# Spacing the feed-forward weight chunks and word buffers 32 bytes further apart

## The chip, the cores and the metric

The kernel runs on one core of a Trainium2 chip. The metric is device time in microseconds (us), as the median of timed runs of the whole program. A core has a matrix engine (PE, with its weight loads shown apart as PEld), a vector engine (DVE), a scalar engine (ACT), a general engine (POOL) and a queue engine that issues DMAs (SP).

## The reference

The program computes a long convolution (as a product of Fourier transforms), gates it with its input, and sends every token through a feed-forward network with squared ReLU:

```python
h_filt = (np.maximum(pos_emb @ w1, 0.0) @ w2) * window      # filter, 12480 x 128
u = x * v                                                   # 4 batches, 12480 x 128
y = irfft(rfft(u, 2 * S) * rfft(h_filt, 2 * S), 2 * S)[:S]
t = (x * y).reshape(49920, 128)
h = np.maximum(t @ w_in, 0.0)                               # 128 x 2048
out = h * h @ w_out                                         # 2048 x 128
```

## The kernel before

The convolution of each of the four batches is done in four stages of small fp32 matrix products (`s1` to `s4`, two-dimensional transforms over a 112 x 112 grid in the buffer `W`). The feed-forward network runs over 98 groups of up to 512 tokens; each group takes eight steps `f`. After the first batch, the transform stages of the next batch are woven between the feed-forward steps: a step issues its products, and in between it advances the generator of the stages by one. Once all batches are transformed, the last stretch (here "the tail", from about 2620 us on) holds feed-forward steps alone.

To keep fp32 accuracy at the speed of the short format, every operand of the feed-forward network is split into a high and a low word (fp32r tiles), and each product is three: high by high, low by high, high by low. That is the helper `mm3`, lines 95, 96 and 97. Its first argument is the stationary operand (loaded into PE by a weight load ahead of the product), its second the moving one:

```python
nc.tensor.matmul(o, lh, rh, start=first, stop=False)   # line 95
nc.tensor.matmul(o, ll, rh, start=False, stop=False)   # line 96
nc.tensor.matmul(o, lh, rl, start=False, stop=last)    # line 97
```

The stationary operands are the feed-forward weights. They lie in 16 chunks `wt[0]` to `wt[15]` of 2048 bytes for each partition, eight of `w_in` and eight of `w_out`; a chunk holds 1024 bytes of high words and 1024 of low words, and `wi(k, h, f)` picks 128 columns of one. A chunk first holds the raw 64-bit weights (tile `raw`, loaded by `load_weights`) and is then overwritten by its converted words (tile `wt`, made by `convert_weights` from temporaries `cv`).

The moving operands are words of tokens, `zh` and `zl` (two buffers each, made by `zsplit`), against `w_in` into PSUM tile `A` (`m_h`), and words of squared activations, `gh` and `gl` (two buffers each, made by `m_g` and `m_l`, 4096 bytes for two sub-tiles), against `w_out` into PSUM tile `O` or, in the tail, `F` (`m_o`). In the tail every odd step takes its `r`, `gh` and `gl` from a second pool `tp` that lies elsewhere, on the left side of memory. One step is twelve products: six `A<-zh/zl` and six `O<-gh/gl`. ACT makes the ReLU and the squares, DVE the low words (line 818), and both run behind PE.

Products of one engine run in the order of the code. While one product streams its moving operand out of SBUF, the load of the next product's weights is running. Two reads of SBUF are therefore always going on at the same time: the moving words of this product and the weights of the next. Below, the *offset* of a product is the SBUF byte address of the weights that are loaded under it minus that of its own moving words, modulo 256.

Of the kernel before, what the change touches and what calls it, by code (L numbers as in the profile page):

```python
# [8 lines left out]
F32R = mybir.dt.float32r  # L9
F16 = mybir.dt.float16  # L10
I32 = mybir.dt.int32
# [5 lines left out]
D = 128  # L17
# [9 lines left out]
GT = NT // NG  # L27
NS = NF // 2
GM = 512
# [9 lines left out]
TH = 4  # L39
CW = 256  # L40
NCW = DFF // CW


@with_exitstack
def hyena_moe_kernel(
# [34 lines left out]
    def pool(name, side="left", **kw):  # L80
        return tc.tile_pool(name=name, bufs=kw.pop("bufs", 2), side=side, reuse_waits="tile", **kw)
# [17 lines left out]
    def load_weights(wp):  # L99
        raws = []  # L100
        for c in range(2 * NCW):
            raw = wp.tile([128, CW, 2], I32, tag="w", name="raw", bufs=2 * NCW)
            src = (w_in if c < NCW else w_out).bitcast(I32)[:, c % NCW * 2 * CW : (c % NCW + 1) * 2 * CW]
            nc.sync.dma_start(out=raw.rearrange("p a b -> p (a b)"), in_=src)
            raws.append(raw)
        return raws

    def convert_weights(p, wp, raws, wt, chunks):
        V = nc.vector
        for c in chunks:  # L110
            low, high = raws[c][:, :, 0], raws[c][:, :, 1]
            mag, top, sgn = (p.tile([128, CW], I32, tag=k, name="cv") for k in ("cm", "ct", "cs"))
            mf = mag.bitcast(F32)
            tf = top.bitcast(F32)
            V.tensor_scalar(out=top, in0=high, scalar1=0x7FFFFFFF, scalar2=None, op0=ALU.bitwise_and)
            yield
            V.tensor_scalar(out=mf, in0=tf, scalar1=2.0**-15, scalar2=122880.0, op0=ALU.max, op1=ALU.min)
            yield
            V.tensor_scalar(out=top, in0=mag, scalar1=3, scalar2=0x7FFFFFFF, op0=ALU.logical_shift_left, op1=ALU.bitwise_and)
            yield  # L120
            V.tensor_scalar(out=mag, in0=low, scalar1=1, scalar2=None, op0=ALU.logical_shift_right)
            nc.gpsimd.tensor_copy(mf, mag)
            yield
            V.tensor_scalar(out=sgn, in0=high, scalar1=-0x80000000, scalar2=0x40000000, op0=ALU.bitwise_and, op1=ALU.bitwise_xor)
            yield
            V.tensor_tensor(out=top, in0=top, in1=sgn, op=ALU.bitwise_xor)
            wt[c] = wp.tile([128, 2, CW], F32R, tag="w", name="wt", bufs=2 * NCW)
            hi12, lo12 = wt[c][:, 0, :], wt[c][:, 1, :]
            nc.gpsimd.tensor_copy(hi12, tf)
            yield  # L130
            V.tensor_scalar(out=sgn, in0=top, scalar1=-0x800000, scalar2=None, op0=ALU.bitwise_and)
            yield
            V.scalar_tensor_tensor(out=mf, in0=mf, scalar=2.0**-51, in1=sgn.bitcast(F32), op0=ALU.mult, op1=ALU.mult)
            yield
            V.tensor_sub(out=tf, in0=tf, in1=hi12.bitcast(F32))
            yield
            V.tensor_add(out=lo12, in0=tf, in1=mf)
            yield
# [546 lines left out]
    def run(gen):  # L685
        for _ in gen:
            pass
# [6 lines left out]
    def take(name, *args, **kw):  # L694
        held[name] = ExitStack()
        return held[name].enter_context(pool(name, *args, **kw))
# [39 lines left out]
    wp = ctx.enter_context(pool("wp", "right"))  # L736
    wt = {}
    tabs = [take(k, "right").tile([128, TH * TC, 2, I], F32, name=k, bufs=1) for k in ("tbb", "tba")]
    for k in range(2 * TH):
        table(t2h, k, tabs[k < TH])  # L740
    raws = load_weights(wp)
    run(s1f)
    s1 = stage1(0, True, "right", during_s1)
    cvp = take("cvp")
    conv = [convert_weights(cvp, wp, raws, wt, range(k, 2 * NCW, 2)) for k in range(2)]
    run(stage2(True, True, "left", during_s2f))
    ft = []
# [4 lines left out]
    held["tbb"].close()  # L752

    mp = ctx.enter_context(pool("mp", "right"))
    head = [mp.tile([D, GM], F32R, tag=k, name=k)[:, :GT] for k in ("zh", "zl")]
    s4 = stage4(0, done, take("t1p"))
    run(stage3(True, ft[0], lambda t: t == -12 and step(s4)))
    idle(12)
# [1 line left out]
    def wi(k, h, f):  # L760
        return wt[k * NCW + f // 2][:, h, f % 2 * 128 : (f % 2 + 1) * 128]

# [13 lines left out]

    def zsplit(zi):
        n = zi.shape[1]
        hi = mp.tile([D, GM], F32R, tag="zh", name="zh")[:, :n]
        lo = mp.tile([D, GM], F32R, tag="zl", name="zl")[:, :n]  # L780
        nc.scalar.copy(hi, zi)  # L781
        nc.gpsimd.tensor_sub(out=lo, in0=zi, in1=hi.bitcast(F32))  # L782
        return hi, lo
# [7 lines left out]
    def m_g(A, p, n, between, way):  # L791

        r = p.tile([128, 2, GM], F32, tag="r", name="r")[:, :, :n]
        hi = p.tile([128, 2, GM], F32R, tag="gh", name="gh")[:, :, :n]
        h = A[:, :, :n]
        nc.scalar.activation(r, h, AF.Relu)  # L799
        between()  # L800
        if way != "b":
            nc.scalar.activation(hi, r, AF.Square)  # L802
        if way == "p":
            nc.vector.scalar_tensor_tensor(out=h, in0=h, scalar=0.0, in1=r, op0=ALU.max, op1=ALU.mult)  # L804
            return p, h, hi, way
        nc.scalar.activation(r, r, AF.Square)  # L806
        return p, r, hi, way

    def m_l(st, share):
        p, g, hi, way = st  # L810
        lo = p.tile([128, 2, GM], F32R, tag="gl", name="gl")[:, :, : g.shape[2]]
        if way == "b":
            nc.vector.tensor_copy(hi, g)  # L813
        if share:
            nc.gpsimd.tensor_sub(out=lo[:, 1, :], in0=g[:, 1, :], in1=hi[:, 1, :].bitcast(F32))
            nc.vector.tensor_sub(out=lo[:, 0, :], in0=g[:, 0, :], in1=hi[:, 0, :].bitcast(F32))
        else:
            nc.vector.tensor_sub(out=lo, in0=g, in1=hi.bitcast(F32))  # L818
        return hi, lo
# [51 lines left out]
    for i in range(NM):  # L871
        for f in range(NS):
            adv(1)
            A = m_h(zT, f)
            last = m_o(*pend.pop(0)) if len(pend) > 1 else None
            adv(2)
            if not nxt[0] and not tail:
                tail.append(ctx.enter_context(pool("tp")))
            late.append((i, f, m_g(A, tail[0] if tail and f % 2 else mp, GN[i], lambda: m_out(last), way(i * NS + f))))
            while len(late) > len(tail):  # L880
                x, y, st = late.pop(0)
                pend.append((x, y, m_l(st, False)))
            if i + 1 < NM:
                if f == (1 if i else 3):
                    ready(i + 1)
                    zi = zload(i + 1)
                if f == (4 if i else 6):
                    nzT = zsplit(zi)
            adv(3)
            n = i * NS + f  # L890
            if stage[0] != since[0]:
                since = stage[0], n + 4
            owed += EXTRA[done[1] > 0]
            if owed >= 1 and stage[0] in (("s3", "s4") if done[1] else ("s2", "s3", "s4")) and nxt[0] == 1 and n >= since[1]:
                owed -= 1
                since = stage[0], n + 3
                for k in range(1, 4):
                    adv(k)
        if i + 1 < NM:
            zT = nzT  # L900
    for x, y, st in late:
        pend.append((x, y, m_l(st, True)))
# [114 lines left out]
```

## Time and profile before

| | |
|---|---|
| timed runs | 3122.88, 3111.55, 3119.26 us; median 3119.26 us |
| profiled execution, first to last instruction | 3112.0 us (the only time that the profile gives for it) |
| PE busy | 3072.7 us, 99% of the span |
| PEld, DVE, ACT, POOL busy | 83%, 82%, 78%, 48% |
| chain that ended last | PE 92% |
| granted TensorE clock | 0.999 of full speed over the span |

The timed runs are 11 us apart, 0.4% of the time. The busy share of PE counts overlapping products once, so the spacing of the products, not their durations, has to be read to see how fast PE goes. A product's duration runs from its start to the end of its results and is longer than the spacing to the next start (389 against 227 ns in a stretch shown below); a difference of durations between two products of the same shape is a difference of spacing.

### The profile page before, as it was taken

How to read it: one execution, taken by the hardware profiler on the slowest of the kernel's cores; microseconds unless marked ns; L12 is line 12 of the kernel's file. 1: busy time of each engine (PE TensorE's matmuls, PEld its weight loads, DVE VectorE, ACT ScalarE, POOL GpSimd, SP SyncE). 2: the span in 40 equal slices, each digit the busy share in tenths (PEclk: the TensorE clock that was granted, in tenths of full speed). 3: DMA queues.
4: the chain of work that ended last, by engine and by line, in shares of the span. 5: the costliest groups of instructions: out<-in, count | busy, mean ns of one | idle time of the engine just before them, and what ended most of it. 6: DMA issues, size and time to landing. Idle time of an engine off the chain costs nothing.

```text
span 3112.0 us, 49107 instructions
## 1 busy us (share of the span) xinstructions
PE 3072.7 (99%) x16086; PEld 2579.8 (83%) x16086; DVE 2538.0 (82%) x3080; ACT 2419.1 (78%) x3130; POOL 1501.6 (48%) x1631
## 2 busy tenths in 40 slices
PE   9989999999999999999999999999999999999999
PEld 7767888888888888888888888888888888888887
DVE  7888898878877988878877898878877799777776
ACT  5556777777788777788888877787788887878787
POOL 1249765556544565546644575646644466000000
PEclk9999999999999999999999999999999999999999
DMA  5783574434200664434300375434410176100000
GB/s 184 263 294 99 137 166 137 124 111 145 67 21 15 151 161 132 130 91 127 115 15 21 80 176 144 133 92 121 124 51 14 36 168 156 33 24 24 24 26 20
DMA packets 342623, 323.11 MB, mean 104 GB/s; under 512 B 161968, under 2 KB 288800, under 8 KB 342368
## 3 DMA queue, kind: packets, MB, share of 16 engines
q1 hardware_dynamic: 313216, 272.25, 30.2%
q0 software_dynamic: 29152, 47.72, 6.4%
q8 instruction: 128, 2.10, 0.3%
q14 instruction: 127, 1.04, 0.1%
HBM read 231.78 MB, written 65.60 MB: 96 GB/s over the span
## 4 chain that ended last, share of the span: by engine, by line
PE 92%; POOL 2%; DMA 2%; DVE 2%; issue 1%; ACT 1%; SPq 0%; DVEq 0%; ACTq 0%; POOLq 0%
PE A L95 11%; PE A L97 11%; PE A L96 11%; PE O L97 9%; PE O L96 9%; PE O L95 9%; PE F L380 6%; PE F L492 6%; PE F L293 5%; PE F L97 4%; PE F L95 4%; PE F L96 4%; PE A L290 2%; PE A L291 1%; POOL W L405 1%
## 5 line engine op out<-in xcount | busy, mean ns | idle before, releaser
L799 ACT ACTIVATE r<-A 128x1024 f32<-128x1024 f32 (+2 forms) x784 | 803.8, 1025 | 420.8 <-PE A L97 407.0
L818 DVE TENSOR_TENSOR gl<-r,gh 128x1020 fp32r<-128x1020 f32 (+1 forms) x433 | 642.5, 1484 | 113.9 <-ACT r L806 80.0
L95 PE MATMUL A<-zh,wt 128*128 128x512 f32 (+2 forms) x1568 | 671.4, 428 | 0.9 <-DVE gl L818 0.9
L97 PE MATMUL A<-zl,wt 128*128 128x512 f32 (+2 forms) x1568 | 613.8, 391 | 0.0
L96 PE MATMUL A<-zh,wt 128*128 128x512 f32 (+2 forms) x1568 | 612.9, 391 | 0.0
L802 ACT ACTIVATE gh<-r 128x1024 fp32r<-128x1024 f32 (+2 forms) x461 | 486.9, 1056 | 62.8 <-PE O L96 57.2
L97 PE MATMUL O<-gl,wt 128*128 128x512 f32 (+2 forms) x1248 | 487.4, 391 | 4.2 <-DVE gl L818 4.2
L96 PE MATMUL O<-gh,wt 128*128 128x512 f32 (+2 forms) x1248 | 485.0, 389 | 0.0
L95 PE MATMUL O<-gh,wt 128*128 128x512 f32 (+2 forms) x1248 | 484.9, 389 | 0.0
L804 DVE SCALAR_TENSOR_TENSOR A<-A,r 128x1024 f32<-128x1024 f32 (+2 forms) x350 | 425.4, 1215 | 68.1 <-ACT r L799 66.5
L818 DVE TENSOR_TENSOR gl<-A,gh 128x1024 fp32r<-128x1024 f32 (+2 forms) x350 | 426.1, 1218 | 63.1 <-ACT gh L802 20.4
L806 ACT ACTIVATE r<-r 128x1020 f32<-128x1020 f32 (+1 forms) x434 | 460.3, 1061 | 12.5
L813 DVE CAST gh<-r 128x1020 fp32r<-128x1020 f32 (+1 forms) x323 | 225.6, 698 | 221.2 <-ACT r L806 152.7
L782 POOL TENSOR_TENSOR zl<-zi,zh 128x512 fp32r<-128x512 f32 (+2 forms) x97 | 126.4, 1303 | 522.4 <-ACT zh L781 506.1
L567 POOL TENSOR_TENSOR al<-W,ah 112x512 fp32r<-112x512 f32 x214 | 281.9, 1318 | 189.2 <-ACT ah L561 185.0
L501 POOL TENSOR_TENSOR W<-c 112x224 f32<-112x224 f32 x256 | 217.6, 861 | 285.7 <-ACT c L499 275.0
L97 PEld LDWEIGHTS A<-zl,wt 128*128 128x128 f32 x1568 | 294.6, 188 | 64.7
L95 PEld LDWEIGHTS A<-zh,wt 128*128 128x128 f32 x1568 | 295.5, 188 | 51.4 <-DVE gl L818 3.1
L96 PEld LDWEIGHTS A<-zh,wt 128*128 128x128 f32 x1568 | 296.2, 189 | 45.1
L417 POOL TENSOR_TENSOR W<-W,m 112x256 f32<-112x256 f32 x168 | 177.8, 1058 | 247.3 <-DVE m L415 233.1
L97 PEld LDWEIGHTS O<-gl,wt 128*128 128x128 f32 x1248 | 234.2, 188 | 54.5 <-DVE gl L818 5.9
L96 PEld LDWEIGHTS O<-gh,wt 128*128 128x128 f32 x1248 | 234.2, 188 | 50.6
(127 smaller groups left out, 5495.3 us busy)
## 6 DMA issues: line engine op xcount, KB each, us to landing
ht<-Hd SPq DMA_DIRECT2D x224, 256.0 KB
tb<-t POOLq DMA_DIRECT2D x224, 196.0 KB, 3.1
xt<-x SPq DMA_DIRECT2D x224, 112.0 KB
xt<-xs SPq DMA_DIRECT2D x96, 224.0 KB
vt<-vs SPq DMA_DIRECT2D x96, 224.0 KB
tb<-t2s SPq DMA_DIRECT2D x168, 112.0 KB
Hd<-he SPq DMA_DIRECT2D x28, 512.0 KB
zd<-zs SPq DMA_DIRECT2D x222, 64.0 KB
```

Of the source, the lines that this page charges most:

```text
L95: nc.tensor.matmul(o, lh, rh, start=first, stop=False)
L96: nc.tensor.matmul(o, ll, rh, start=False, stop=False)
L97: nc.tensor.matmul(o, lh, rl, start=False, stop=last)
L380: nc.tensor.matmul(U[:I, k * 256 : (k + 1) * 256], tb[:KP, k, :], a[:, k], start=True, stop=True)
L501: nc.gpsimd.tensor_sub(out=dst[:, 1], in0=c[:, :, 0:3:2], in1=c[:, :, 3:0:-2])
L567: eng.tensor_sub(out=lo, in0=w, in1=hi.bitcast(F32))
L799: nc.scalar.activation(r, h, AF.Relu)
L802: nc.scalar.activation(hi, r, AF.Square)
L804: nc.vector.scalar_tensor_tensor(out=h, in0=h, scalar=0.0, in1=r, op0=ALU.max, op1=ALU.mult)
L806: nc.scalar.activation(r, r, AF.Square)
L813: nc.vector.tensor_copy(hi, g)
L818: nc.vector.tensor_sub(out=lo, in0=g, in1=hi.bitcast(F32))
```

## The change

`WP = 8` words (32 bytes) are added behind each of the first 15 weight chunks, behind each `zh` and `zl` buffer and behind each `gh` and `gl` buffer. So that a chunk keeps its place, the 16 buffers of one ring become 16 rings of one buffer each. The views into the tiles are those of before, so every instruction reads and writes the same shapes.

```diff
+WP = 8
 ...
-            raw = wp.tile([128, CW, 2], I32, tag="w", name="raw", bufs=2 * NCW)
+            raw = wp.tile([128, 2 * CW + WP * (c < 2 * NCW - 1)], I32, tag=f"w{c}", name="raw", bufs=1)[:, : 2 * CW].rearrange("p (a b) -> p a b", b=2)
 ...
-            wt[c] = wp.tile([128, 2, CW], F32R, tag="w", name="wt", bufs=2 * NCW)
+            wt[c] = wp.tile([128, 2 * CW + WP * (c < 2 * NCW - 1)], F32R, tag=f"w{c}", name="wt", bufs=1)[:, : 2 * CW].rearrange("p (a b) -> p a b", a=2)
 ...
-    head = [mp.tile([D, GM], F32R, tag=k, name=k)[:, :GT] for k in ("zh", "zl")]
+    head = [mp.tile([D, GM + WP], F32R, tag=k, name=k)[:, :GT] for k in ("zh", "zl")]
 ...
-        hi = mp.tile([D, GM], F32R, tag="zh", name="zh")[:, :n]
-        lo = mp.tile([D, GM], F32R, tag="zl", name="zl")[:, :n]
+        hi = mp.tile([D, GM + WP], F32R, tag="zh", name="zh")[:, :n]
+        lo = mp.tile([D, GM + WP], F32R, tag="zl", name="zl")[:, :n]
 ...
-        hi = p.tile([128, 2, GM], F32R, tag="gh", name="gh")[:, :, :n]
+        hi = p.tile([128, 2 * GM + WP], F32R, tag="gh", name="gh")[:, : 2 * GM].rearrange("p (t n) -> p t n", t=2)[:, :, :n]
 ...
-        lo = p.tile([128, 2, GM], F32R, tag="gl", name="gl")[:, :, : g.shape[2]]
+        lo = p.tile([128, 2 * GM + WP], F32R, tag="gl", name="gl")[:, : 2 * GM].rearrange("p (t n) -> p t n", t=2)[:, :, : g.shape[2]]
```

In the built programs the addresses, modulo 256, come out so:

| buffers | before | after |
|---|---|---|
| weight chunks 0 to 7 (`w_in`) and 8 to 15 (`w_out`) | all 224 | 0, 32, 64, ... 224 for each eight |
| `zh`, `zl` (two buffers each) | all 224 | 0 and 32, 64 and 96 |
| `gh`, `gl` (two buffers each) | all 224 | 128 and 160, 192 and 224 |
| `gh`, `gl` of the tail's second pool | all 128 | 128 and 160, 192 and 224 |
| everything else on the right side (tables and buffers of the first stages, `r`, `zi`, `ot`) | | moved by 32 modulo 256 as a whole |

There are 8861 feed-forward products that are followed by another feed-forward product. Counted in the built program, their offsets are:

| offset | 0 | 32 | 64 | 96 | 128 | 160 | 192 | 224 |
|---|---|---|---|---|---|---|---|---|
| before | 8364 | 0 | 0 | 497 | 0 | 0 | 0 | 0 |
| after | 1514 | 683 | 1483 | 763 | 1486 | 679 | 1485 | 768 |

No instruction moves on any engine. On PE, at one of the places where a step's products against `w_out` (`gh`, `gl`) are followed by a product of stage 4 (`ah`, `tb`), before:

```order
L95 MATMUL O<-gh,wt 128x510
L96 MATMUL O<-gh,wt 128x510
L97 MATMUL O<-gl,wt 128x510
L95 MATMUL O<-gh,wt 128x510
L96 MATMUL O<-gh,wt 128x510
L97 MATMUL O<-gl,wt 128x510
L95 MATMUL F<-ah,tb 112x256
```

The changed program has the same rows in the same places, each with a line number that is one higher; the other engines agree in the same way. What differs is which engines a few instructions wait for, since chunks now lie in other places over memory that the filter's first stage has left. On SP, the loads of the raw chunks before:

```order
L104 DMA raw<-w_in 128x512 [waits DMAHW4_49]
L104 DMA raw<-w_in 128x512 [waits DMAHW5_49,PE_49,Activation_49]
L104 DMA raw<-w_in 128x512 [waits DMAHW6_49]
L104 DMA raw<-w_in 128x512 [waits DMAHW7_49,Pool_49]
L104 DMA raw<-w_in 128x512 [waits DMAHW0_49]
L104 DMA raw<-w_in 128x512 [waits DMAHW1_49]
```

The same six loads after the change:

```order
L105 DMA raw<-w_in 128x512 [waits DMAHW4_49]
L105 DMA raw<-w_in 128x512 [waits DMAHW5_49]
L105 DMA raw<-w_in 128x512 [waits DMAHW6_49]
L105 DMA raw<-w_in 128x512 [waits DMAHW7_49]
L105 DMA raw<-w_in 128x512 [waits DMAHW0_49,DVE_49,PE_49]
L105 DMA raw<-w_in 128x512 [waits DMAHW1_49,Pool_49]
```

The waits for PE, ACT and POOL have moved from the second and fourth load to the fifth and sixth; the queue's order is that of before.

## Rows read from the trace of the kernel before

**Rows 1.** The page: span, busy engines, granted clock, chain by engine.

```profile
span 3112.0 us, 49107 instructions
...
PE 3072.7 (99%) x16086; PEld 2579.8 (83%) x16086; DVE 2538.0 (82%) x3080; ACT 2419.1 (78%) x3130; POOL 1501.6 (48%) x1631
...
PEclk9999999999999999999999999999999999999999
...
PE 92%; POOL 2%; DMA 2%; DVE 2%; issue 1%; ACT 1%; SPq 0%; DVEq 0%; ACTq 0%; POOLq 0%
```

**Rows 2.** Groups of PE by line: busy us, mean ns of one, idle before.

```profile
L95 PE MATMUL A<-zh,wt 128*128 128x512 f32 (+2 forms) x1568 | 671.4, 428 | 0.9 <-DVE gl L818 0.9
L97 PE MATMUL A<-zl,wt 128*128 128x512 f32 (+2 forms) x1568 | 613.8, 391 | 0.0
...
L97 PE MATMUL O<-gl,wt 128*128 128x512 f32 (+2 forms) x1248 | 487.4, 391 | 4.2 <-DVE gl L818 4.2
L96 PE MATMUL O<-gh,wt 128*128 128x512 f32 (+2 forms) x1248 | 485.0, 389 | 0.0
L95 PE MATMUL O<-gh,wt 128*128 128x512 f32 (+2 forms) x1248 | 484.9, 389 | 0.0
...
L96 PE MATMUL F<-gh,wt 128*128 128x510 f32 x320 | 125.5, 392 | 0.0
```

**Rows 3.** Who PE waited for: us in total, times, longest.

```profile
PE F L380 <- DVE W L387: 7.9, 23, 2.2
```

**Rows 4.** PE in order of time: start, duration; six 512-column products at offset 0.

```profile
1004.61 0.39 PE L95 MATMUL O<-gh,wt 128*128 128x512 f32 x1
...
1005.98 0.26 PE L492 MATMUL F<-ft,v 112*112 112x112 f32 x1
```

**Rows 5.** PE in order of time, tail: six products at offset 96, then six at 0.

```profile
2900.59 0.40 PE L95 MATMUL F<-gh,wt 128*128 128x510 f32 x1
...
2901.99 0.39 PE L95 MATMUL A<-zh,wt 128*128 128x510 f32 x1
...
2903.36 0.39 PE L95 MATMUL F<-gh,wt 128*128 128x510 f32 x1
...
2904.72 0.39 PE L95 MATMUL A<-zh,wt 128*128 128x510 f32 x1
```

**Rows 6.** Groups of PE at 397.1, 909.8, 499.25, 1022.3 us: one product each.

```profile
L97 PE MATMUL O<-gl,wt 128*128 128x512 f32 x1 | 0.4, 396 | 0.0
...
L97 PE MATMUL O<-gl,wt 128*128 128x512 f32 x1 | 0.4, 391 | 0.0
...
L97 PE MATMUL O<-gl,wt 128*128 128x512 f32 x1 | 0.4, 397 | 0.0
...
L97 PE MATMUL O<-gl,wt 128*128 128x512 f32 x1 | 0.4, 389 | 0.0
```

**Rows 7.** In order of time at 503.33 us: a last product, the load beneath.

```profile
503.33 0.40 PE L97 MATMUL O<-gl,wt 128*128 128x512 f32 x1
503.33 0.61 PEld L293 LDWEIGHTS F<-ef,ut 112*120 112x120 f32 x3
```

**Rows 8.** Groups of PE at 1936.3, 2025.7, 1978.9, 1907.8, 2080.7 us: one product each.

```profile
L97 PE MATMUL O<-gl,wt 128*128 128x510 f32 x1 | 0.4, 389 | 0.0
...
L97 PE MATMUL O<-gl,wt 128*128 128x510 f32 x1 | 0.4, 395 | 0.0
...
L97 PE MATMUL O<-gl,wt 128*128 128x510 f32 x1 | 0.4, 388 | 0.0
...
L97 PE MATMUL O<-gl,wt 128*128 128x510 f32 x1 | 0.4, 387 | 0.0
...
L97 PE MATMUL O<-gl,wt 128*128 128x510 f32 x1 | 0.4, 397 | 0.0
```

**Rows 9.** Tile raw, by operation: duration min/median/max, first and last start.

```profile
L115 DVE TENSOR_SCALAR cv<-raw x16: 285/286/290, 85.5 to 137.4; 128x256 int32<-128x256 int32 x16
...
L104 SPq DMA_DIRECT2D raw<-w_in x8: 328/352/431, 24.0 to 38.5; - x8
```

## The prediction

> **What bounds the kernel now.** I read the page first, then the groups by line, the waits, and last the order of time. [...] The wait of PE that is longest in total is 7.9 us [rows 3], and for the low words of the squares it waited only 4.2 us in the whole program [rows 2]. So what counts is how closely PE's own products follow each other. The groups by line show of what kind they are: 3 x (1568 + 1248 + 320) = 9,408 feed-forward products [rows 2]. A nanosecond on each of them is 9.4 us.
>
> The order of time shows their spacing. In a stretch between two transforms, six products of 512 columns take 1005.98 - 1004.61 = 1.37 us, some 228 ns each [rows 4]. [...]
>
> [...] The kernel before has one place where the offset is not 0: the odd steps of the tail, whose `gh` and `gl` lie at residue 128 while the weights are at 224, offset 96. There six products of 510 columns take 2901.99 - 2900.59 = 1.40 us, and in the next step, same shapes, same weights, offset 0, 2904.72 - 2903.36 = 1.36 us [rows 5]. That is 233 against 227 ns. The group of these products has a mean of 392 ns, where those of the untouched buffers have 389 [rows 2]: half of the 320 at some 395, half at 388 or 389. So the spacing does depend on the offset, and offset 0, which the kernel has almost everywhere, is the better of the two.
>
> [...]
>
> More offsets are seen once a step, where the last product runs while the first weights of a transform, which lie elsewhere, are loaded. Its duration against the 389 ns of its neighbours shows what the one offset costs:
> - Offset 32, 512 columns: 396 and 391 ns (78 and 92 such) [rows 6]; I take 393.5.
> - Offset 64: 397 ns at 512 columns, all of 42 [rows 6]; 389 or 395 at 510, 11 and 10 of 21 [rows 8]. I take 394.5, the middle of 397 and 392.
> - Offset 96: 6.7 ns over offset 0 at 510 columns, so 388 + 7 = 395 [rows 5, 8].
> - Offset 160: 389 ns at 512 columns, 130 such [rows 6]; 387 or 397 at 510, 50 and 28 [rows 8]. I take 390.5.
> - Offset 192: 397 ns at 512 columns, 22 such, shown by one with its load (0.40 in time order) [rows 7]; 388 at 510, 10 of 11 [rows 8]. I take 392.5.
> - Offsets 128 and 224 are not in this trace for these shapes. Their nearest rows are the five above, mean 393.2 ns, which I take; the ends are the lowest and highest of those rows, 387 and 397.
> - Offset 0: 390.5 ns, the mean over the groups [rows 2] without the first product of a step, whose 428 holds the change from a transform. It is above the 389 of a settled stretch, since after each transform some products run longer.
>
> **The sum.** With the counts after the change (of 8,861: 1514, 683, 1483, 763, 1486, 679, 1485, 768 for offsets 0 to 224), the additions over 390.5 ns are 683 x 3.0 + 1483 x 4.0 + 763 x 4.5 + 1486 x 2.7 + 679 x 0 + 1485 x 2.0 + 768 x 2.7 = 20.5 us. Before, the 497 products at offset 96 are already in the 390.5, so nothing is taken off. PE is the chain, and its waits are too short to swallow more than a little: I count all of it. The sum is a difference to the profiled execution of 3112.0 us, which is 7 us under the median of the timed runs; put on the median, 3119.3 + 20.5 is 3140 us.
>
> Bounds: with the lower row of each offset (391, 389, 395, 387, 388, and 387 for the two unknown) the same sum is about -12 us, so 3107; with the upper rows (396, 397, 395, 397, 397, 397, 397) it is about +46 us, so 3165.
>
> **What costs nothing.** The raw loads keep their place on SP; a wait for the filter's last readers moves by a few loads. They were issued from 24.0 us on, in 0.4 us each, and the first conversion reads one at 85.5 us [rows 9], so a delay of tens of microseconds is hidden by the filter's stages; if that cover went, it would be the conversions on DVE that start late, in a stretch that is a tenth of the span. The tables and buffers of the first stages keep their offsets to each other; only products between them and `W` shift by 32, 224 products of two passes in the program, 3 us at the 7 ns of above. ACT and DVE now read `r`, `gh` and `gl` at different residues instead of one. If that slowed them by a few per cent, they would still be behind PE: with 82% busy, DVE has 500 us to spare. GpSimd and the DMAs read none of the padded buffers in a loop that PE waits for.
>
> **Rivals.**
> *No change.* Products settle: after a transform the same offset 0 gives durations up to 397 ns for some products and then falls to 389. If what is lost depends more on how the two reads happened to start than on the offset, a mix of offsets costs what a mix of starts costs, and the gain and the loss cancel: 3119 us. For it: offset 160 has 387 and 397 at one width, and 64 and 192 differ between 510 and 512 columns [rows 6 to 8]. Against it: offset 96 kept its 6.7 ns through whole steps [rows 5]. [...]
> [...]
> *The change isn't there.* The addresses of the built program exclude it.
>
> **Chances.** Forecast (20 us more, 3140): 0.58. No change: 0.27. Faster: 0.15. Half a per cent, 16 us, is about what a measurement of this kernel can tell from no change. The forecast's own range is 3122 to 3165. The range that holds the time 8 times in 10 is 3104 to 3166: it takes in both bounds of the sum and the case of no change, and leaves out most of the faster case. Slower by over 0.5%: 0.57; within: 0.28; faster: 0.15.
>
> **What would show it.** If right, the groups `A<-zh`, `A<-zl`, `O<-gh`, `O<-gl` have means some 2 ns higher, the steady stretches no longer have one spacing but one that goes with the chunk (that is with `f`), and steps whose offset happens to be 0 still run at 227 ns. The tail's even steps get slower and its odd steps not. DVE and ACT have more idle time, no new wait of PE appears, and the first 330 us stay. It would be wrong if offsets 128 and 224 lie under 389 ns, if the products after a change of offset lose their delay, or if ACT or DVE became so much slower that PE waits for `gl`.

## The result, and the profile after

The changed kernel takes 3139.11 us (median of five runs, 3134.80 to 3140.66), the kernel before 3119.26 us (3111.55 to 3122.88). The ratio is 1.0069, with a 95% interval of 1.0053 to 1.0085: slower by 0.7%, 20 to 21 us.

The page of the changed kernel answers to [rows 1]:

```profile
span 3137.3 us, 49114 instructions
...
PE 3099.7 (99%) x16086; PEld 2588.5 (83%) x16086; DVE 2541.5 (81%) x3080; ACT 2417.4 (77%) x3130; POOL 1497.5 (48%) x1631
...
PEclk9999999999999999999999999999999999999999
...
PE 91%; DVE 3%; DMA 2%; POOL 2%; issue 1%; ACT 1%; SPq 1%; DVEq 0%; ACTq 0%; POOLq 0%
```

The span is 25 us longer and PE is busy for 27 us more. Its weight loads (PEld) run beneath the products: before as after, one takes 188 ns, where the products of a settled stretch start 227 ns apart, so a product has a load beneath it for most of its time, not always. They are up by 9 us in all; DVE, ACT and POOL are busy as long as before within 5 us. The seven instructions more are semaphore instructions in the queues of SP, DVE and ACT. The groups of PE by line show where the time lies (line 95 of before is 96 here, and so on); they answer to [rows 2]:

```profile
L96 PE MATMUL A<-zh,wt 128*128 128x512 f32 (+2 forms) x1568 | 675.2, 431 | 0.7 <-DVE gl L819 0.6
L98 PE MATMUL A<-zl,wt 128*128 128x512 f32 (+2 forms) x1568 | 616.1, 393 | 0.0
L97 PE MATMUL O<-gh,wt 128*128 128x512 f32 (+2 forms) x1248 | 490.8, 393 | 0.0
L98 PE MATMUL O<-gl,wt 128*128 128x512 f32 (+2 forms) x1248 | 490.5, 393 | 4.1 <-DVE gl L819 4.1
L96 PE MATMUL O<-gh,wt 128*128 128x512 f32 (+2 forms) x1248 | 489.9, 393 | 0.0
L493 PE MATMUL F<-ft,v 112*112 112x112 f32 x1792 | 212.6, 267 | 2.9 <-POOL v L480 2.2 <-DVE W L501 0.6
L381 PE MATMUL F<-W,tb 120*112 120x256 f32 x672 | 170.3, 378 | 0.3 <-PE O L98 0.3
```

The last two rows are products of the transforms. Before, they read:

```profile
L492 PE MATMUL F<-ft,v 112*112 112x112 f32 x1792 | 212.4, 267 | 3.2 <-POOL v L479 2.5 <-DVE W L500 0.6
L380 PE MATMUL F<-W,tb 120*112 120x256 f32 x672 | 170.2, 378 | 0.0
```

The feed-forward groups `A` and `O` are 2 to 4 ns longer for each product. These two groups of the transforms are what they were; one smaller one, `F<-W,tbb`, went from 404 to 413 ns, 1.3 us of busy time. Before, the transforms also show what a split into words gains: an f32 product of 256 columns, `F<-W,tb`, is two rows of the trace some 215 ns apart, 430 ns, and the three products of words on as many columns, `F<-ah,tb` and `F<-al,tb`, are three rows some 119 ns apart, 357 ns. The wait for `gl` is 4.1 us, where it was 4.2. In the tail, the starts of five half steps of six products each, which answer to [rows 5]:

```profile
2911.40 0.39 PE L96 MATMUL A<-zh,wt 128*128 128x510 f32 x1
...
2912.77 0.39 PE L96 MATMUL F<-gh,wt 128*128 128x510 f32 x1
...
2914.17 0.39 PE L96 MATMUL A<-zh,wt 128*128 128x510 f32 x1
...
2915.57 0.40 PE L96 MATMUL F<-gh,wt 128*128 128x510 f32 x1
...
2916.98 0.39 PE L96 MATMUL A<-zh,wt 128*128 128x510 f32 x1
```

Six products take 1.37, 1.40, 1.40 and 1.41 us in succession: the 1.36 us of the even steps before is gone.

From here on, *excess* is the start-to-start spacing of two feed-forward products less a fixed amount for the columns of the first: 213.3 ns at 512, 212.5 at 510, 185.8 at 446. The expectations call that amount streaming time. It is my assumption, and no run shows a product that takes just this; it serves as the zero of a scale on which widths can be set side by side, and what is measured is the differences between excesses. Between two widths the trace of before bears it out: in settled stretches products of 512 columns start 227 ns apart and those of 446 columns 200, a difference of 27 ns where the amounts differ by 27.5. In the settled stretch of [rows 4] the excess is 14 ns. Elsewhere it is a mean over the trace. Left out are some 420 of 8831 pairs (30 less than the built program's count, all of them at offset 0) whose excess is over 60 ns, nearly all of them the first product of a step behind a transform; together they had 72.9 us of it before and 73.8 after, so they carry almost nothing of the difference. The excess was 15.5 ns at offset 0 and 20.4 ns at offset 96 before, over all products 15.8. After, it is 18.5.

### The profile page after: what moved, and what is told of

Same layout as the page of the kernel before. It is cut to its first block, busy times and chain, and to the rows that moved or that the text cites. A ratio compares the mean times of both kernels' runs of the same rounds, so it can differ in the third digit from the quotient of the medians.

```text
span 3137.3 us, 49114 instructions
## 1 busy us (share of the span) xinstructions
PE 3099.7 (99%) x16086; PEld 2588.5 (83%) x16086; DVE 2541.5 (81%) x3080; ACT 2417.4 (77%) x3130; POOL 1497.5 (48%) x1631
## 4 chain that ended last, share of the span: by engine, by line
PE 91%; DVE 3%; DMA 2%; POOL 2%; issue 1%; ACT 1%; SPq 1%; DVEq 0%; ACTq 0%; POOLq 0%
PE A L96 11%; PE A L97 11%; PE A L98 11%; PE O L98 9%; PE O L97 9%; PE O L96 9%; PE F L381 6%; PE F L493 5%; PE F L294 5%; PE F L96 4%; PE F L98 4%; PE F L97 4%; PE A L291 2%; PE A L292 1%; POOL W L406 1%
## 5 line engine op out<-in xcount | busy, mean ns | idle before, releaser
L819 DVE TENSOR_TENSOR gl<-r,gh 128x1020 fp32r<-128x1020 f32 (+1 forms) x433 | 646.7, 1493 | 114.1 <-ACT r L807 79.5
L97 PE MATMUL O<-gh,wt 128*128 128x512 f32 (+2 forms) x1248 | 490.8, 393 | 0.0
L96 PE MATMUL O<-gh,wt 128*128 128x512 f32 (+2 forms) x1248 | 489.9, 393 | 0.0
L807 ACT ACTIVATE r<-r 128x1020 f32<-128x1020 f32 (+1 forms) x434 | 459.8, 1059 | 12.5
```

## The experiments

The theory that the prediction rested on (A) is that the value of the offset sets the excess. Its first rival (B) is that any steady offset settles, and that the change costs because the offset now differs from one product to the next. Each run is compared with the kernel before on the same chip: 3114.13 us for the first four, then 3113.72, and 3114.20 for the last two. That is some 5 us less than the 3119.26 us of above, which several expectations start from, so the differences are what to compare.

**One fixed offset, 128.** The word buffers as a whole lie lower, and nothing is spaced:

```diff
+    padp = ctx.enter_context(pool("padp", "right"))
+    padp.tile([128, 32], F32, name="pad", bufs=1)
     mp = ctx.enter_context(pool("mp", "right"))
```

> All buffers are those of the kernel before, but the word buffers as a whole lie 128 bytes lower, so that 8334 of the 8861 pairs have the one offset 128 instead of 0. Theory A (the value of the offset sets the spacing): in the changed kernel's trace, products at offset 128 were spaced 3.3 ns wider than those at offset 0 of the kernel before (18.8 against 15.5 ns over their streaming time), so 8334 x 3.3 = 27 us more than before, 3147 us. Theory B (what costs is that the offset changes from one product to the next, so that the spacing never settles): one fixed offset settles like offset 0 does, 3119 us within 6.

Measured: 3143.83 us, ratio 1.0098 (1.0081 to 1.0115). That is 30 us more than before, where A expected 27. The excess at offset 128 is 19.3 ns, and it doesn't settle lower: 19.1 ns at 512 columns, 19.5 at 510.

**One fixed offset, 64.** The same with a pad of 16 words.

> The same with 64 bytes, offset 64 for 8334 pairs. Theory A by the changed kernel's trace (17.6 against 15.5 ns): 8334 x 2.1 = 18 us more, 3137 us; by the prediction's own value for this offset, 4 ns, 33 us more. Theory B: 3119 us within 6.

Measured: 3151.42 us, ratio 1.0123 (1.0105 to 1.0140), excess 20.4 ns. The time went the way that A says, but by 37 us, twice the 18 that the changed kernel's trace had given and close to the prediction's 33. The groups of PE by line, against [rows 2]:

```profile
L95 PE MATMUL A<-zh,wt 128*128 128x512 f32 (+2 forms) x1568 | 676.7, 432 | 0.7 <-DVE gl L820 0.6
L97 PE MATMUL A<-zl,wt 128*128 128x512 f32 (+2 forms) x1568 | 620.4, 396 | 0.0
L97 PE MATMUL O<-gl,wt 128*128 128x512 f32 (+2 forms) x1248 | 492.4, 395 | 4.2 <-DVE gl L820 4.2
L96 PE MATMUL O<-gh,wt 128*128 128x512 f32 (+2 forms) x1248 | 491.8, 394 | 0.0
L95 PE MATMUL O<-gh,wt 128*128 128x512 f32 (+2 forms) x1248 | 491.7, 394 | 0.5 <-DVE gh L815 0.5
```

Each of these groups is 4 to 5 ns up, with an offset that changes 165 times in the whole program, as often as before. Theory B expected 3119 us in both runs and falls.

**The weight chunks alone.** The first two changed lines of the diff, without those of the word buffers.

> Only the weight chunks are spaced by 32 bytes, the word buffers are not. All eight offsets occur about 1100 times each, but within the six products against one chunk the offset stays the same: it changes 1156 times from one product to the next, against 5118 in the changed kernel and 165 before. Theory A (mean over the offsets): about the changed kernel, 3135 to 3142 us. Theory B: a quarter of the changed kernel's loss or less, 3120 to 3127 us.

Measured: 3137.97 us, ratio 1.0078 (1.0063 to 1.0093), 24 us more.

**The word buffers alone.** The other changed lines, without those of the chunks.

> Only the word buffers are spaced by 32 bytes, the weight chunks all keep one residue. All eight offsets occur, unevenly, and the offset changes 5098 times from one product to the next, as in the changed kernel. Theory A and theory B both expect the changed kernel's time here, 3135 to 3142 us; the two runs with parts of the change together say which part carries the loss.

Measured: 3137.14 us, ratio 1.0073 (1.0058 to 1.0088), 23 us more. Each half of the change by itself costs what both cost together. With the weights alone the offset changes 1156 times and with the words alone 5098 times, and the loss is the same. So the loss does not grow with the number of changes, as B would have it. The two runs have different mixes of offsets, though, and a change is not without effect: in the changed kernel the products at offset 0 whose predecessor was at 0 too have an excess of 16.7 ns, the others 17.8, while at offset 64 it is the other way round, 18.8 against 16.7.

The run with the weights alone also tells which weights count. Where the last of six products runs over the load of the next chunk, its own weights and the loaded ones lie at different offsets. Sorted by the offset of the loaded ones, the excess of these products is lowest at 192 (16.0 ns) and high at 128 and 160 (20.6 and 20.5), about as for all products of that run (16.8, 19.8 and 20.6). Sorted by their own weights it isn't: 20.8 at 192, 18.4 at 160, some 124 products for each. The agreement is rough; at 64 and 96 these products are 2 ns off the others (20.2 against 18.1, 18.1 against 20.2). It speaks for the load beneath a product, as the prediction had assumed, and not for the weights in use.

**Weights and words moved together.** The same pad of 32 words, placed ahead of the weights' pool:

```diff
+    padp = ctx.enter_context(pool("padp", "right"))
+    padp.tile([128, 32], F32, name="pad", bufs=1)
     wp = ctx.enter_context(pool("wp", "right"))
```

> Weight chunks and word buffers both lie 128 bytes lower, so that every offset is 0 as before (the tail's second pool, which stays, has 224 instead of 96). The word buffers have just the addresses that they had in the run with offset 128. Theory A (the difference of the two addresses counts): the time before, 3114 to 3119 us. Rival C (the residue of the word buffers itself counts, whatever the weights do): the time of the run with offset 128, 3144 us.

Measured: 3112.85 us, ratio 0.9994 (0.9984 to 1.0003). The word buffers have exactly the addresses of the first experiment, which was 1% slower; with the weights moved along, nothing is lost. Rival C falls: the difference counts, not the residue. This also leaves no room for the engines that write and read the words: their addresses are those of the slow run, and what differs is the address of the weights, which once they are converted only PE's loads read.

**One fixed offset, 192.** A pad of 48 words.

> One fixed offset of 192 for 8334 pairs. Theory A, with the value that this offset had in the run with the weights alone spaced (16.8 ns over the streaming time against 15.5 before): 8334 x 1.3 = 11 us more than before, 3125 us. If any offset other than 0 costs the same: 3144 to 3151 us as for 128 and 64.

Measured: 3133.64 us, ratio 1.0067 (1.0050 to 1.0084), excess 17.7 ns. That is 20 us more than before, between offset 0 and the others; A expected 11, and a price that is the same for every offset 30 to 37. Neither is met: the offsets differ, but the price from the run with mixed offsets was too low here as for 64.

**An offset of 240, which is no multiple of 32.** `zh`, `zl`, `gh` and `gl` get 64 words more, and their views start at word 4.

> The words start 16 bytes into their buffers (which are 256 bytes longer each), offset 240 for 8334 pairs: is the cost a matter of steps of 32 bytes, or finer? If what counts is which 32 bytes the two reads touch, 16 bytes less than offset 0 gives either the 15.5 ns of offset 0 or the 18.3 ns of offset 224 (3119 or 3142 us); if it varies smoothly, something between them, 17 ns, 3131 us.

Measured in a single run: 3142.44 us, 29 us more, excess 18.9 ns. Sixteen bytes away from offset 0, a loss as large as at 128 is already there. The words of this run are also the only ones that start at no multiple of 32 bytes, so it does not tell whether the distance or that start costs.

**A shorter load.** What if the load beneath a product has only half the columns?

```diff
-        nc.tensor.matmul(o, ll, rh, start=False, stop=False)
+        nc.tensor.matmul(o[:64] if half else o, ll[:, :64] if half else ll, rh, start=False, stop=False)
```

> Buffers as before. The second product of each three (low words of the weights by high words) uses 64 of its 128 stationary columns, so the low words of the weights are left out for half of the outputs; the load that runs under the first product of each three is then half as long. Theory A (the load's reads hold up the words' reads): the first products against w_out, 389 ns before, lose about half of the 14 ns that they run over their streaming time, 382 ns. Rival D (the 14 ns are not from the load): they stay at 389 ns.

Measured in a single run: 3114.26 us. The groups by line (in the second row, 64 stationary columns):

```profile
L97 PE MATMUL O<-gl,wt 128*128 128x512 f32 (+2 forms) x1248 | 488.3, 391 | 3.9 <-DVE gl L818 3.8
L96 PE MATMUL O<-gh,wt 128*64 128x512 f32 (+2 forms) x1248 | 487.1, 390 | 0.0
L95 PE MATMUL O<-gh,wt 128*128 128x512 f32 (+2 forms) x1248 | 485.9, 389 | 0.0
```

The first products, line 95, stand at 389 ns as before. The halved loads take 134 ns in the trace, the whole ones 188, so they are shorter by 54 ns and not half as long. My expectation, 382, was wrong: at offset 0 these products are no closer together with the shorter load. Elsewhere in the same run the load does show: the 497 products at offset 96 in the tail, whose addresses are those of before, fell from 20.4 to 17.6 ns.

**A shorter load at offset 64.** Both edits together, to see whether what an offset adds scales with it.

> The halved load of the run before (low words of the weights left out for half of the outputs) together with the fixed offset 64, where the first products against w_out had a mean of 394 ns and the whole kernel 3151 us. The halved load alone left the 389 ns of offset 0 as they were. Theory F (some 14 ns are there whatever is loaded, and only what an offset adds to them comes from the two reads meeting): the first products, under the halved load, lose the larger part of their 5 ns, 390 to 391 ns, the second and third stay at 394 to 395. Rival G (the load beneath has nothing to do with it): the first products stay at 394 ns like the others.

Measured in a single run: 3130.11 us, against 3151 with the whole load at this offset. The same groups:

```profile
L97 PE MATMUL O<-gl,wt 128*128 128x512 f32 (+2 forms) x1248 | 492.3, 394 | 4.0 <-DVE gl L820 4.0
L95 PE MATMUL O<-gh,wt 128*128 128x512 f32 (+2 forms) x1248 | 489.8, 392 | 0.0
L96 PE MATMUL O<-gh,wt 128*64 128x512 f32 (+2 forms) x1248 | 489.7, 392 | 0.0
```

Neither F nor G is borne out. A third of the loads is shorter and over half of what the offset had cost is gone (16 us more than before instead of 37), so the load has a part in it; but it is gone from the second products as much as from the first, and almost all of it in groups of 510 columns (mean excess 15.9 ns against 20.9), with 512 columns still at 20.1. The edit also halves the outputs of the second products, which is a change of the products and not only of their loads. Whether it is the two reads that hold each other up, and how, is not settled by this.

**Offset 0 everywhere.** The kernel before with the tail's second pool brought to the weights' residue:

```diff
                 tail.append(ctx.enter_context(pool("tp")))
+                tail[0].tile([128, 24], F32, name="pad", bufs=1)
```

> The kernel before, with the tail's second pool 96 bytes further up, so that all 8861 pairs have offset 0. The 497 products that had 20.4 ns over their streaming time should come to the 15 ns of the others: 497 x 5.4 = 2.7 us less than before, 3111 us; the group of products F in the tail from 392 to 389 ns. If the offset did not set the spacing, no change in that group.

Measured: 3109.26 us against 3114.20, ratio 0.9981 (0.9972 to 0.9990), eleven runs. One of the tail's three groups `F`:

```profile
L96 PE MATMUL F<-gh,wt 128*128 128x510 f32 x320 | 124.2, 388 | 0.0
```

The other two have the same numbers. The three come from 391 to 392 ns (one of them in [rows 2]) to 388: some 3.6 ns on 960 products, 3.5 us. The gain, 4.9 us between the medians, is more than the 2.7 expected. The 497 products that were at offset 96 fell further than foreseen, from 20.4 to 14.2 ns (3.1 us), and the `A` products of the same odd steps, whose offset had been 0 all along, fell from 16.7 to 14.2 (1.2 us): what a product loses depends on the offsets of its neighbours too. This version is faster than both kernels, and it goes the other way from the change: it makes offsets equal.

## Why the prediction was right, point by point

**The bound.** PE's own products set the time, before and after: PE is busy for 99% of the span in both and has 92 and 91% of the chain. The busy times of the nine feed-forward groups rise by 25 us in sum, the span by 25.3 us, and no wait of PE grew by more than 2 us. Nothing was swallowed, as the sum had assumed.

**Whether addresses matter.** Shown, by the fixed offsets of 128, 64 and 192 (1.0%, 1.2% and 0.7% slower), and by the run that moves both sides (no change). It had been argued from one pair of steps in the tail [rows 5], and that pair told true: without the odd offset there, those products take 388 ns.

**The sum.** The prediction added 20.5 us on the median; 19.9 us was measured between the medians. That these agree within 1 us is luck: the timed runs lie 11 us apart before and 6 after, and the profiled executions, for which the sum was worked out, differ by 25.3 us, so the sum is a fifth short. The single terms were less good than their sum. In ns over offset 0 of the kernel before (15.5), for the prediction's additions, for runs with one fixed offset, for the run with the weights alone, and for the changed kernel:

| offset | 0 | 32 | 64 | 96 | 128 | 160 | 192 | 224 |
|---|---|---|---|---|---|---|---|---|
| predicted | 0 | 3.0 | 4.0 | 4.5 | 2.7 | 0 | 2.0 | 2.7 |
| one fixed offset | 0 | | 4.9 | 4.9 (tail of before) | 3.8 | | 2.2 | |
| weights alone | 1.1 | 4.5 | 2.6 | 4.7 | 4.3 | 5.1 | 1.3 | 2.8 |
| changed kernel | 2.0 | 4.8 | 2.1 | 3.4 | 3.3 | 4.1 | 3.6 | 2.2 |

With the counts of the changed kernel, its own row makes 26.7 us; less the 497 x 4.9 = 2.4 us that the tail had before, 24.3 us, against a span that grew by 25.3. The term that failed most is the price of offset 160. It was taken as nothing, from last products of a step [rows 6, 8], whose loads were those of a transform with 112 columns, and it costs 4 to 5 ns (2.8 us with the count). Likewise wrong was that products at offset 0 keep their 227 ns: in the changed kernel they have 2 ns more (3.0 us). That the products around them do this is borne out by the `A` products of the tail (16.7 to 14.2 ns when their neighbours' offset went), but was not tested in this mix. Offset 192 cost 5.3 us instead of 3.0. Against that, offset 64 cost half of what I took (3.1 instead of 5.9 us), though by itself it is dearer (4.9). So the errors cancel in part, and the sum came close because a mean over all offsets is sounder than any single price. The rows also show what theory A leaves out: an offset has no one price, but one that depends on the offsets around it (64: 4.9, 2.6 and 2.1 ns).

**What was to cost nothing.** The first feed-forward product begins at 333.61 us, before at 332.88. The raw loads are issued from 25.5 us on (24.0 before) and first read at 85.5 us, as in [rows 9]. DVE's subtractions `gl<-r` went from a mean of 1484 to 1493 ns, 4 us in all, and DVE's busy share fell from 82 to 81%.

**The rivals.** *No change* lost: products do settle, but at a level that goes with the offset (excess 15.5 ns at offset 0 before, 17.7, 19.3 and 20.4 ns with one fixed offset of 192, 128 and 64). The same products with the same loads are up to 1.2% of the program apart (3151.42 us at offset 64, 3114.13 before). What they lose this time to is not shown. *Faster*, a time under that of before, had a chance of 0.15 and lost: the mean of the groups (without the first products of a step) did not fall under 389 ns, it rose from 390.3 to 393.1. The offsets unknown then are no cheaper than the rest (128: 3.8 ns alone, 224: 2.2 to 2.8 in the mixes).

**What would have shown it.** The groups' means (up by 2 to 4 ns, 2 expected) and the tail's even steps (excess of `gh` and `gl` from 14.2 to 19.3 ns) came out as said; the tail's odd steps fell from 20.4 to 18.9. That the spacing goes with the chunk is plain with the weights alone spaced (means of 15.9 to 20.2 ns over the eight `f` for the products against `w_out`), but hardly in the changed kernel, where the words move too (17.6 to 19.0). Steps at offset 0 did not keep their 227 ns.

## What to carry to other kernels

When a matrix engine is the bound and its products follow each other without a wait, see whether their spacing is the same for buffers that lie differently: the kernel's own odd place (here the tail's second pool, 233 against 227 ns) gives a first price of a layout before anything is changed. Spreading addresses was no improvement in itself here: equal residues of the moving words and of the weights loaded beneath them were the best of all that were tried, and each of the other layouts cost 0.7 to 1.2%: one offset of 64, 128, 192 or 240 for nearly all products, or a mix. If the prices of single cases are read from few instances, or always at the same place in a sequence, trust their mean more than each.

## What the runs showed of the hardware that was not expected

Products settled into a pattern, not into one spacing. In the tail, where PE has nothing but feed-forward products, the excess depends on the place of a product in its six, and at each place of the cases below it repeats from step to step within half a nanosecond (standard deviation). With offset 0 everywhere, places alternate between 12.5 and 15.5 to 16.0 ns, mean 14.2. In the even steps of the run with offset 192 every place has 17.5. In those with offset 64 the excess runs through 19, 22.5 and 27.5 in turn. Before, five of the six products at offset 96 had 20.8 to 21.7 ns and the fourth 15.8. A price therefore has to be read over the whole pattern. The prediction read several from the last product of a step alone, always the same place; that this is what misled it at 160 is likely but not tested.

With the weight load shortened from 188 to 134 ns, the first products against `w_out` at offset 0 keep their 389 ns. What an offset adds, on the other hand, did shrink when a third of the loads were shortened, but at 510 columns (20.9 to 15.9 ns) and not at 512 (20.1 both times). The products of 512 columns all run before some 1930 us and those of 510 after, so the two columns need not be what decides. What does, and why a shift of the words by 16 bytes costs as much as one by 128 (18.9 and 19.3 ns), stays open.
